# Channel 0 of b as a three-row product on TensorE, the copy of b's E on ScalarE, and two buffers for the products

## The chip, the cores and the metric

The kernel runs on one core of a Trainium2 chip. The metric is device time in microseconds of one execution, lower is better. The core's engines are TensorE (PE in the profile; PEld is its weight load), VectorE (DVE), ScalarE (ACT), GpSimd (POOL) and SyncE (SP), whose queue issues most transfers.

## The reference

The input x has 8 x 3072 x 256 numbers. Three stages follow each other:

```python
X = np.fft.fft(np.fft.fft(x, axis=1), axis=2).real    # stage 1
t = X.reshape(B * S, D)
t = ((t @ w_a) * (t @ w_b)) @ w_out                   # stage 2, F = 1536
# stage 3: 8 experts, the one with the largest logit per token
h = np.maximum(t[mask] @ w1[e], 0.0)
out[mask] = gate * (h @ w2[e])
```

## The kernel before, in words

The kernel makes use of a symmetry of the Fourier transform over the sequence: position s and position -s have spectra over the 256 channels whose even parts agree and whose odd parts differ in sign. So stages 1 and 2 work on a half of the positions: there are 24 tiles of 512 positions (t = 0 to 23), and each product gives the rows of two positions. UV holds the transformed input of a batch, Wt the weights w_a and w_b after the same turn, both as a high and a low fp16 part. Wt[:, ab, uv, a] has 128 partitions for w_a (ab = 0) and w_b (ab = 1), for the even (uv = 0) and the odd part (uv = 1), high (a = 0) and low (a = 1).

The even part has 129 channels, one more than the partitions. The one that is left over, channel 0, sits in partition 0 of the odd part. It has to be taken out of the odd product and belongs to the even one. The kernel before does it on VectorE: x's row of that channel is spread over 128 partitions by two one-row matmuls per tile (line 817, kept in st_x), the weight's row is turned into one number per partition (w0, by ab_row), and x * w0 is added to the even product E, once for a and once for b (line 861).

The work goes by steps: for each tile twelve steps f, each for 128 of the 1536 columns of w_a and w_b, 288 in all. The order of all engines' instructions is written out by hand. In a step TensorE makes the even products (six matmuls with 512 columns, three for a and three for b, into banks s[0] and s[1]), then the second product of a step three back with w_out (24 matmuls with 256 columns, line 894), and then the odd products into the same banks (line 828 both times). Around it stand:

- first(): ScalarE copies b's bank to BP (line 834), VectorE makes AM, the first half of hf, and b minus (lines 835 to 837), for the step before;
- the pair of line 861 on VectorE, which moves E of a and of b from the banks of this step to EE, with channel 0 added. The odd products may not start before;
- first_minus(): VectorE makes the other half of hf (line 840);
- second(): ScalarE rounds hf to fp16 in hl (line 845), GpSimd makes the rest (line 847).

The products' tiles hf come from a pool of three buffers. from64_sizes takes its scratch tiles from the same pool while weights are converted in the setup. Other work is dealt into the steps by a planner with a budget per engine and step: Fourier products of later batches (line 662), folding x on GpSimd, splitting the expert weights, and for each tile, after its second products, the normalisation of rows (lines 930, 941, 947), transposes on SP's queue, the gate, and eight scatters on GpSimd. After the steps the expert stage follows, which the change doesn't touch. mini_rows does one extra tile of eight positions with small matmuls (line 771).

Of the kernel before, what the change touches and what calls it, by code (L numbers as in the profile page):

```python
# [8 lines left out]
FP32 = mybir.dt.float32  # L9
FP16 = mybir.dt.float16  # L10
BF16 = mybir.dt.bfloat16
I32 = mybir.dt.int32
ACTF = mybir.ActivationFunctionType
ALU = mybir.AluOpType
# [4 lines left out]
B, S, D = 8, 3072, 256  # L19
F = 1536  # L20
# [21 lines left out]
def chain_kernel(ctx, tc, x, x384, w_a, w_b, w_out, w_gate, w_og, w1, w2, dft, c16, c32, ids, out):  # L42
    nc = tc.nc
    w_a, w_b, w_out = (w.bitcast(I32).rearrange("a (b c) -> a b c", c=2) for w in (w_a, w_b, w_out))
    pe, act, dve, pool, sp = nc.tensor, nc.scalar, nc.vector, nc.gpsimd, nc.sync
# [34 lines left out]
    UV = place_at(H2, FP16, [2, 4, F], "p (a b c) -> p a b c", a=2, b=4)  # L80
    Wt = place_at(H2 + 24576, FP16, [2, 2, 2, F], "p (a b c d) -> p a b c d", a=2, b=2, c=2)
    wo = place_at(H2 + 49152, FP16, [NF, 2, D], "p (a b c) -> p a b c", a=NF, b=2)
    UVm = place_at(H2 + 64512, FP16, [4, 128], "p (a b) -> p a b", a=4)
# [15 lines left out]
    one = es.enter_context(tc.tile_pool(name="one", bufs=1))  # L99
    two = es.enter_context(tc.tile_pool(name="two", bufs=2))  # L100
    three = es.enter_context(tc.tile_pool(name="three", bufs=3))
# [4 lines left out]
    w0 = one.tile([128, 2, NF], FP32, name="w0")  # L106
# [20 lines left out]
    EE = one.tile([128, 2, 512], FP32, name="EE")  # L127
# [4 lines left out]
    sel = place_at(H2 + 60992, FP32, [48], None)[0:4 * B]  # L132
    junk = place_at(H2 + 63488, BF16, [2, D], "p (a d) -> p a d", a=2)
    AM = one.tile([128, 2, 512], FP32, name="AM")
    ohx = one.tile([128, 9, 8], FP16, name="ohx")
    sinv = one.tile([128, 2], FP32, name="sinv")
    Rt = one.tile([128, 12, 2], FP32, name="Rt")
# [29 lines left out]
    def at(u, point, fn):  # L167
        if fn is None:
            return
        todo.setdefault((u, point), []).append(fn)  # L170
# [72 lines left out]
    TINY = 1.125 * 2.0 ** -15  # L243

    def from64_sizes(raws):
        ts = [three.tile([128, 2, 512], I32, tag="hf", name="t64") for _ in raws]
        for t, raw in zip(ts, raws):
            act.activation(out=t[:, 1].bitcast(FP32), in_=raw[:, :, 1].bitcast(FP32), func=ACTF.Abs)
        return ts
# [42 lines left out]
    def ab_low(ab, m, ps):  # L292
        fs = slice(512 * m, 512 * m + 512)
        for uv in range(2):
            dve.scalar_tensor_tensor(out=Wt[:, ab, uv, 1, fs], in0=ps[uv], scalar=sw[ab], in1=Wt[:, ab, uv, 0, fs], op0=ALU.mult, op1=ALU.subtract)

    def ab_row(ab, m, ps):
        for f in range(4 * m, 4 * m + 4):
            for h in range(2):
                pe.matmul(out=ps[:, f:f + 1], lhsT=Wt[0:1, ab, 1, h, 128 * f:128 * f + 128], rhs=ones16[0:1, 0:1], start=(h == 0), stop=(h == 1))  # L300
        act.activation(out=w0[:, ab, 4 * m:4 * m + 4], in_=ps[:, 4 * m:4 * m + 4], func=ACTF.Copy)
# [450 lines left out]
    def mini_rows():  # L752
        st = {}
        n = B * NF
        Bm = place_at(Pb[1], FP32, [n], None)
        hm = place_at(Pb[1] + 4 * n, FP32, [n], None)
        hlm = place_at(Pb[1] + 8 * n, FP16, [2, NF, B], "p (a f n) -> p a f n", a=2, f=NF)

        def clear():
            pool.memset(Ym, 0.0)  # L760
            pool.memset(rowim, 0)
            pool.memset(ohm, 0.0)

        def prod():
            st["s"] = aux()
            for f in range(NF):
                for ab in range(2):
                    o = 128 * ab + B * f
                    for uv in range(2):
                        for i, (a, h) in enumerate(((0, 0), (0, 2), (1, 0))):  # L770
                            pe.matmul(out=st["s"][:, o:o + B], lhsT=Wt[:, ab, uv, a, 128 * f:128 * f + 128], rhs=UVm[:, h + uv, 0:B], start=(uv == 0 and i == 0), stop=(uv == 1 and i == 2))

        def copy_b():
            act.activation(out=Bm, in_=st["s"][:, 128:128 + n], func=ACTF.Copy)

        def times():
            dve.scalar_tensor_tensor(out=hm, in0=st["s"][:, 0:n], scalar=CA * CA, in1=Bm, op0=ALU.mult, op1=ALU.mult)

        def hi():
            act.activation(out=hlm[:, 0].rearrange("p f n -> p (f n)"), in_=hm, func=ACTF.Copy)  # L780

        def lo():
            dve.tensor_tensor(out=hlm[:, 1].rearrange("p f n -> p (f n)"), in0=hm, in1=hlm[:, 0].rearrange("p f n -> p (f n)"), op=ALU.subtract)

        def sums():
            st["y"] = aux()[0:B, 0:D]
            for f in range(NF):
                for i, (a, h) in enumerate(((0, 0), (1, 0), (0, 1))):
                    pe.matmul(out=st["y"], lhsT=hlm[:, h, f, :], rhs=wo[:, f, a, :], start=(f == 0 and i == 0), stop=(f == NF - 1 and i == 2))

        def copy_y():
            act.activation(out=Ym[0:B, 0, :], in_=st["y"], func=ACTF.Copy)

        return [
            (0, [("pool", 1.0, clear)]),
            (1, [("pe", 1, prod), ("act", 0.25, copy_b), ("dve", 0.2, times)]),
            (1, [("act", 0.25, hi), ("dve", 0.5, lo)]),
            (1, [("pe", 1, sums), ("act", 0.4, copy_y)]),
        ]
# [3 lines left out]
    st_x = {}  # L803
    prev = []

    def aux():
        return cur["aux"][0]
# [5 lines left out]
    def x_items(t):  # L813
        def spread():
            st_x["ps", t] = aux()
            for i, k in enumerate((1, 3)):
                pe.matmul(out=st_x["ps", t], lhsT=ones16[0:1, :], rhs=UV[0:1, (t // 3) % 2, k, 512 * (t % 3):512 * (t % 3) + 512], start=(i == 0), stop=(i == 1))

        def keep_x():
            st_x[t] = xes[t % 2]  # L820
            act.activation(out=st_x[t], in_=st_x["ps", t], func=ACTF.Copy)

        return [(0, [("pe", 1, spread), ("act", 0.6, keep_x)])]

    def products(s, src, fs, uv):
        for ab in range(2):
            for i, (a, h) in enumerate(((0, 0), (0, 2), (1, 0))):
                pe.matmul(out=s[ab], lhsT=Wt[:, ab, uv, a, fs], rhs=src[:, h + uv, :], start=(uv == 0 and i == 0), stop=(i == 2), skip_group_check=(uv == 1))  # L828

    def first(P):  # L830

        a, b = P["s"]
        P["hf"] = three.tile([128, 2, 512], FP32, tag="hf", name="hf")
        act.activation(out=BP, in_=b, func=ACTF.Copy)  # L834
        dve.scalar_tensor_tensor(out=AM[:, 0, :], in0=EE[:, 0, :], scalar=2.0, in1=a, op0=ALU.mult, op1=ALU.subtract)  # L835
        dve.scalar_tensor_tensor(out=P["hf"][:, 0, :], in0=a, scalar=CA * CA, in1=BP, op0=ALU.mult, op1=ALU.mult)  # L836
        dve.scalar_tensor_tensor(out=b, in0=EE[:, 1, :], scalar=2.0, in1=b, op0=ALU.mult, op1=ALU.subtract)  # L837
# [12 lines left out]
    def step(T, f, job):  # L850
        src = tile_src(T)
        fs = slice(128 * f, 128 * f + 128)
        s, cur["aux"] = SB[cur["n"] % 2], SB[(cur["n"] + 1) % 2]
        cur["n"] += 1
        run("sp")
        P = {"s": s, "T": T, "f": f}
        products(s, src, fs, 0)
        if prev:
            first(prev[0])
        for ab in range(2):  # L860
            dve.scalar_tensor_tensor(out=EE[:, ab, :], in0=st_x[T[0]], scalar=w0[:, ab, f:f + 1], in1=s[ab], op0=ALU.mult, op1=ALU.add)  # L861
        if prev:
            first_minus(prev[0])
        run("early")
        if job:
            g, i, k = job
            ps = dft_products(g, i, bank_beside(k))
            dft_out(g, i, ps)
            if i == 11:
                dft_last(g)  # L870
        middle()
        run("act")
        if prev:
            second(prev.pop())
        run("dve0")
        run("dve")
        run("pool0")
        run("pool")
        products(s, src, fs, 1)
        prev.append(P)  # L880

# [307 lines left out]
    for g, G in enumerate(GROUPS):  # L1189
# [4 lines left out]
        for b in G:  # L1194
            for t in range(3 * b, 3 * b + 3):
                ts = [(t, 0, 4)]
# [17 lines left out]
    for u, un in enumerate(plan):  # L1214
        if un[0] == "D":
            first_of.setdefault(un[1], u)
            if pending:
                T, f = pending.pop(0)
                if f == NF - 1:
                    ends[T] = u  # L1220
        else:
            begins.setdefault(un[1], u)
            pending.append((un[1], un[2]))
            if len(pending) > 3:
                T, f = pending.pop(0)
# [28 lines left out]
    with tc.manual_schedule():  # L1254
# [28 lines left out]
        raws = deque()  # L1283
# [28 lines left out]
        flat = [Y[n].rearrange("p a d -> p (a d)") for n in range(4)]  # L1312
# [70 lines left out]
        for m in range(3):  # L1383
            ab_row(0, m, flat[1])
        ab_low(1, 0, [flat[0], flat[2]])
        ab_row(1, 0, flat[1])
        warm(8)
        out_squares(0)
        sizes()
# [16 lines left out]
        for m in range(1, 3):  # L1406
            def late(m=m):
                late_ps.append(cur["aux"])
                ab_turn(1, m, H, late_ps[-1])
            at(m + 1, "pe", late)  # L1410
            at(m + 1, "dve", lambda m=m: ab_low(1, m, late_ps[m - 1]))
            at(m + 2, "pe", lambda m=m: ab_row(1, m, aux()))
            reserve(m + 1, "act", 1.2)
            reserve(m + 1, "dve", 1.2)
        at(4, "pool0", lambda: pool.memset(rows2[:, :, :, 258:264], 0))
# [6 lines left out]
        for T in tiles:  # L1422
            t, j0, _ = T
# [61 lines left out]
        for u, un in enumerate(plan):  # L1485
            if un[0] == "D":
                _, g, i, k, n = un
# [363 lines left out]
```

## Time and profile before

| what | value |
|---|---|
| median of 3 runs | 3058.04 us (3055.01 to 3067.98) |
| profiled execution: its own time | 3057.12 us |
| profiled execution: span | 3055.4 us |
| mean granted TensorE clock | 0.976 of full |
| TensorE, VectorE, ScalarE, GpSimd busy | 2881.0, 2209.5, 1315.1, 1335.7 us |

The profile comes from one execution. Its span is the time from the first to the last instruction; the device time lies a little above it. Busy time is a sum per engine; an engine that is busy most of the time needn't bound each stage.

### The profile page before, as it was taken

The numbers are of one execution on the slowest core, as the hardware profiler recorded it, in microseconds if no ns is written. First come the engines' busy times: TensorE is split into PE (matmuls) and PEld (weight loads), VectorE is DVE, ScalarE is ACT, GpSimd is POOL, SyncE is SP. The second block draws the span as 40 slices with busy tenths as digits, with TensorE's granted clock in tenths as the row PEclk, the third lists the DMA queues.
The fourth block names the chain that finished last, engine by engine and source line by source line (L and its number), as shares of the span: only waits on it lengthen the run. The fifth ranks groups of instructions, "written<-read, shape, count | busy, mean of one in ns | idle before, by whom it ended". The sixth has DMA issues, their size and how long they took to land.

```text
span 3055.4 us, 62396 instructions
## 1 busy us (share of the span) xinstructions
PE 2881.0 (94%) x24101; PEld 2184.9 (72%) x24101; DVE 2209.5 (72%) x4079; ACT 1315.1 (43%) x2605; POOL 1335.7 (44%) x1083
## 2 busy tenths in 40 slices
PE   6899899989999989999989999989999999999998
PEld 4466666656666756666666666678888888888898
DVE  8779699688999688999777998744555555555556
ACT  4454455545455445455444454432333333333332
POOL 6466587365775455775333445413211111111112
PEclk7899999999999999999999999999999999999999
DMA  5421722541221541221452212363222222222211
GB/s 190 118 60 43 177 74 60 145 107 40 77 76 47 137 116 46 77 72 46 99 126 84 77 50 82 87 186 98 58 51 51 50 53 52 51 53 51 51 44 35
DMA packets 363577, 244.48 MB, mean 80 GB/s; under 512 B 303101, under 2 KB 320669, under 8 KB 362382
## 3 DMA queue, kind: packets, MB, share of 16 engines
q1 hardware_dynamic: 342158, 184.75, 24.5%
q0 software_dynamic: 18816, 51.54, 4.9%
q10 hardware_dynamic: 2304, 4.20, 0.5%
q8 instruction: 188, 3.08, 0.4%
q14 instruction: 111, 0.91, 0.1%
HBM read 106.60 MB, written 70.33 MB: 58 GB/s over the span
## 4 chain that ended last, share of the span: by engine, by line
PE 75%; DVE 11%; issue 7%; DMA 3%; ACT 2%; POOL 0%; SPq 0%; DVEq 0%; POOLq 0%; ACTq 0%
PE s L828 19%; PE y L894 18%; PE g L1598 16%; PE g L1622 15%; PE s L662 3%; DVE EE L861 2%; DVE s L837 2%; DVE rows L947 1%; DVE hf L840 1%; DMA big<-in_dft_dram 1%; DVE AM L835 1%; DMA rows<-rows,di 1%; PE s L962 1%; ACT BP L834 1%; PE s L289 1%
## 5 line engine op out<-in xcount | busy, mean ns | idle before, releaser
L828 PE MATMUL s<-big 128*128 128x512 f16 x3456 | 824.9, 389 | 74.1 <-DVE EE L861 66.8
L847 POOL TENSOR_TENSOR hl<-hf,hl 128x1024 f16<-128x1024 f32 x288 | 626.4, 2175 | 566.2 <-ACT hl L845 422.9
L894 PE MATMUL y<-big,hl 128*128 128x256 f16 x6912 | 821.6, 273 | 1.0 <-POOL hl L847 1.0
L894 PEld LDWEIGHTS <-hl 128*128 128x128 f16 x6912 | 672.8, 98 | 152.0 <-issue 12.2
L828 PEld LDWEIGHTS <-big 128*128 128x128 f16 x3456 | 344.2, 100 | 448.4 <-issue 118.2
L1625 POOL DMA_INDIRECT out_dram<-o,di x189 | 195.4, 1034 | 777.3 <-ACT o L1624 524.8
L845 ACT ACTIVATE hl<-hf 128x1024 f16<-128x1024 f32 x288 | 303.8, 1055 | 499.2 <-DVE hf L840 434.3
L1598 PE MATMUL g<-yt,w1t 128*128 128x256 f16 (+1 forms) x4704 | 492.8, 265 | 3.5 <-DVE w1t L1579 3.5
L1622 PE MATMUL g<-w2t,hh 128*128 128x256 f16 x2896 | 479.5, 273 | 0.0
L1598 PEld LDWEIGHTS <-w1t 128*128 128x128 f16 x4704 | 432.0, 98 | 50.1 <-DVE w1t L1579 3.8
L1601 DVE SCALAR_TENSOR_TENSOR hl<-g,hh 128x512 f16<-128x512 f32 x378 | 260.3, 691 | 240.8 <-ACT hh L1600 239.9
L1622 PE MATMUL g<-w2t,hl 128*128 128x256 f16 x1448 | 394.7, 273 | 0.0
L1600 ACT ACTIVATE hh<-g 128x512 f16<-128x512 f32 x378 | 225.3, 598 | 276.3 <-PE g L1598 276.3
L1622 PEld LDWEIGHTS <-hh 128*128 128x128 f16 x3024 | 295.0, 98 | 33.7
L1050 POOL DMA_INDIRECT rows<-rows,di x192 | 191.7, 998 | 264.4 <-DMA rows<-rows,di 199.2
L836 DVE SCALAR_TENSOR_TENSOR hf<-s,BP 128x512 f32<-128x512 f32 x288 | 198.3, 688 | 112.9 <-ACT BP L834 102.7
L1583 DVE COPY w2t<-big 128x4104 f16 x98 | 120.5, 1229 | 206.7 <-PE g L1622 206.7
L1624 ACT ACTIVATE o<-g,sc 128x256 f32<-128x256 f32 x189 | 89.7, 474 | 409.6 <-PE g L1622 360.5
L835 DVE SCALAR_TENSOR_TENSOR AM<-EE,s 128x512 f32<-128x512 f32 x288 | 195.9, 680 | 30.7 <-PE s L828 28.3
L861 DVE SCALAR_TENSOR_TENSOR EE<-big,w,s 128x512 f32<-128x512 f32 x288 | 201.5, 741 | 0.0
L861 DVE SCALAR_TENSOR_TENSOR EE<-xe,w,s 128x512 f32<-128x512 f32 x288 | 201.4, 740 | 0.0
L834 ACT ACTIVATE BP<-s 128x512 f32<-128x512 f32 x288 | 170.2, 591 | 67.6 <-PE s L828 64.3
(332 smaller groups left out, 3039.5 us busy)
## 6 DMA issues: line engine op xcount, KB each, us to landing
big<-in_x_dram SPq DMA_DIRECT2D x48, 514.0 KB
big<-in_dft_dram SPq DMA_DIRECT2D x60, 384.0 KB
big<-in_moe_w_dram SPq DMA_DIRECT2D x16, 1024.0 KB
wsc<-big SPq DMA_DIRECT2D x32, 512.0 KB
big<-wsc SPq DMA_DIRECT2D x7, 2050.0 KB
big<-in_dft_dram SPq DMA_DIRECT2D x60, 192.0 KB
big<-wsc ACTq DMA_DIRECT2D x16, 256.2 KB
raw<-in_moe_w_out_dram SPq DMA_DIRECT2D x6, 512.0 KB
```

Source lines behind the costliest of these rows:

```text
L828: pe.matmul(out=s[ab], lhsT=Wt[:, ab, uv, a, fs], rhs=src[:, h + uv, :], start=(uv == 0 and i == 0), stop=(i == 2), skip_group_check=(uv = ...
L834: act.activation(out=BP, in_=b, func=ACTF.Copy)
L835: dve.scalar_tensor_tensor(out=AM[:, 0, :], in0=EE[:, 0, :], scalar=2.0, in1=a, op0=ALU.mult, op1=ALU.subtract)
L836: dve.scalar_tensor_tensor(out=P["hf"][:, 0, :], in0=a, scalar=CA * CA, in1=BP, op0=ALU.mult, op1=ALU.mult)
L845: act.activation(out=hl[:, 0], in_=hf, func=ACTF.Copy)
L847: pool.tensor_tensor(out=hl[:, 1], in0=hf, in1=hl[:, 0], op=ALU.subtract)
L861: dve.scalar_tensor_tensor(out=EE[:, ab, :], in0=st_x[T[0]], scalar=w0[:, ab, f:f + 1], in1=s[ab], op0=ALU.mult, op1=ALU.add)
L894: pe.matmul(out=Y[w // 2][:, w % 2, :], lhsT=hl[:, h, pm, 128 * j:128 * j + 128], rhs=wo[:, f, a, :], start=(f == 0 and i == 0 and w % 2 = ...
L1598: pe.matmul(out=ps[:, u, :], lhsT=w[:, a, q, 128 * f:128 * f + 128], rhs=yt[:, 2 * h + q, :], start=(m == 0), stop=(m == 5))
L1600: act.activation(out=hh[:, f0:f0 + nu, :], in_=ps, func=ACTF.Relu)
L1601: dve.scalar_tensor_tensor(out=hl[:, f0:f0 + nu, :], in0=ps, scalar=0.0, in1=hh[:, f0:f0 + nu, :], op0=ALU.max, op1=ALU.subtract)
L1622: pe.matmul(out=ps, lhsT=hx[:, f, ts], rhs=wv[:, a, f, :], start=(m == 0), stop=(m == 3 * NF2 - 1))
```

## The change

Channel 0 of b goes to TensorE. Its product is a sum of three rows: high weight by high x, high weight by low x, low weight by high x. b_row copies the weight's row from Wt to a tile W3 with three partitions (three transfers on SP's queue) and clears it in Wt, so that the odd product no longer contains it. x_rows does the same for x, with three transfers for each tile into X3, which lies in an unused part of AM, or X3m for the extra tile. products then adds a matmul with three rows to the even product of b. E of b needs nothing added and is copied to EE by ScalarE. Channel 0 of a stays as it was. The pool of hf has two buffers instead of three.

```diff
     AM = one.tile([128, 2, 512], FP32, name="AM")
+    X3 = AM[0:3, 1, :].bitcast(FP16).rearrange("p (a n) -> p a n", a=2)
+    W3 = one.tile([3, F], FP16, name="W3")
+    X3m = one.tile([3, 8], FP16, name="X3m")
...
-        ts = [three.tile([128, 2, 512], I32, tag="hf", name="t64") for _ in raws]
+        ts = [two.tile([128, 2, 512], I32, tag="hf", name="t64") for _ in raws]
...
+    def b_row(m):
+
+        fs = slice(512 * m, 512 * m + 512)
+        for i, h in enumerate((0, 0, 1)):
+            sp.dma_start(out=W3[i:i + 1, fs], in_=Wt[0:1, 1, 1, h, fs])
+        dve.memset(Wt[0:1, 1, 1, :, fs], 0.0)
+
+    def x_rows(src, n, dst):
+        for i, h in enumerate((1, 3, 1)):
+            sp.dma_start(out=dst[i:i + 1, 0:n], in_=src[0:1, h, 0:n])
...
         def clear():
+            x_rows(UVm, B, X3m)
...
-                            pe.matmul(out=st["s"][:, o:o + B], lhsT=Wt[:, ab, uv, a, 128 * f:128 * f + 128], rhs=UVm[:, h + uv, 0:B], start=(uv == 0 and i == 0), stop=(uv == 1 and i == 2))
+                            pe.matmul(out=st["s"][:, o:o + B], lhsT=Wt[:, ab, uv, a, 128 * f:128 * f + 128], rhs=UVm[:, h + uv, 0:B], start=(uv == 0 and i == 0), stop=(ab == 0 and uv == 1 and i == 2))
+                    if ab:
+                        pe.matmul(out=st["s"][:, o:o + B], lhsT=W3[:, 128 * f:128 * f + 128], rhs=X3m[:, 0:B], start=False, stop=True)
...
         def keep_x():
+            x_rows(UV[:, (t // 3) % 2, :, 512 * (t % 3):512 * (t % 3) + 512], 512, X3[:, t % 2])
...
-    def products(s, src, fs, uv):
+    def products(s, src, fs, uv, x3=None):
...
-                pe.matmul(out=s[ab], lhsT=Wt[:, ab, uv, a, fs], rhs=src[:, h + uv, :], start=(uv == 0 and i == 0), stop=(i == 2), skip_group_check=(uv == 1))
+                pe.matmul(out=s[ab], lhsT=Wt[:, ab, uv, a, fs], rhs=src[:, h + uv, :], start=(uv == 0 and i == 0), stop=(i == 2 and (uv == 1 or ab == 0)), skip_group_check=(uv == 1))
+            if ab and not uv:
+                pe.matmul(out=s[ab], lhsT=W3[:, fs], rhs=x3, start=False, stop=True)
...
-        P["hf"] = three.tile([128, 2, 512], FP32, tag="hf", name="hf")
+        P["hf"] = two.tile([128, 2, 512], FP32, tag="hf", name="hf")
...
-        products(s, src, fs, 0)
+        products(s, src, fs, 0, X3[:, T[0] % 2, :])
...
-        for ab in range(2):
-            dve.scalar_tensor_tensor(out=EE[:, ab, :], in0=st_x[T[0]], scalar=w0[:, ab, f:f + 1], in1=s[ab], op0=ALU.mult, op1=ALU.add)
+        dve.scalar_tensor_tensor(out=EE[:, 0, :], in0=st_x[T[0]], scalar=w0[:, 0, f:f + 1], in1=s[0], op0=ALU.mult, op1=ALU.add)
+        act.activation(out=EE[:, 1, :], in_=s[1], func=ACTF.Copy)
...
-        ab_row(1, 0, flat[1])
+        b_row(0)
...
-            at(m + 2, "pe", lambda m=m: ab_row(1, m, aux()))
+            at(m + 2, "pe", lambda m=m: b_row(m))
```

## Rows read from the trace of the kernel before

**Rows 1.** The page, part 1: busy time, share of the span, instructions.
```profile
PE 2881.0 (94%) x24101; PEld 2184.9 (72%) x24101; DVE 2209.5 (72%) x4079; ACT 1315.1 (43%) x2605; POOL 1335.7 (44%) x1083
```

**Rows 2.** Busy time by stretches: PE, PEld, DVE, ACT, POOL, clock, DMA share, GB/s.
```profile
86.00:1975.00 1889.00, 1768.60 (x13571) 1200.51 (x13571) 1583.73 (x3067) 934.00 (x1902) 1064.09 (x813) 0.98 0.32 84
...
2060.00:3055.00 995.00, 982.81 (x9456) 885.28 (x9453) 520.79 (x805) 310.93 (x561) 204.38 (x199) 1.00 0.23 55
```

**Rows 3.** The chain that ended last, 715 to 730 us: start, us, what.
```profile
718.93 2.59 PE s L828 x12
721.52 2.62 PE y L894 x24
```

**Rows 4.** Waits, 86 to 1975 us: us in total, times, longest us.
```profile
PE s L828 <- DVE EE L861: 66.8, 34, 6.1
```

**Rows 5.** Timelines of VectorE and TensorE, 762 to 802 us: start, us, instructions.
```profile
784.47 7.48 DVE L947 SCALAR_TENSOR_TENSOR rows<-tail,r,rows 128x256 f16<-128x256 f32 x3
...
795.11 4.72 PE L828 MATMUL s<-big 128*128 128x512 f16 x12 [6.09 <-DVE EE L861]
```

**Rows 6.** Timeline of all engines, 715 to 738 us.
```profile
720.20 2.14 POOL L847 TENSOR_TENSOR hl<-hf,hl 128x1024 f16<-128x1024 f32 x1 [3.09 <-ACT hl L845]
720.33 0.60 ACT L834 ACTIVATE BP<-s 128x512 f32<-128x512 f32 x1 [0.21 <-PE s L828]
...
721.03 0.69 DVE L836 SCALAR_TENSOR_TENSOR hf<-s,BP 128x512 f32<-128x512 f32 x1 [0.28 <-ACT BP L834]
...
721.64 0.69 DVE L837 SCALAR_TENSOR_TENSOR s<-EE,s 128x512 f32<-128x512 f32 x1
...
722.24 1.40 DVE L861 SCALAR_TENSOR_TENSOR EE<-big,w,s 128x512 f32<-128x512 f32 x2
...
723.55 0.68 DVE L840 SCALAR_TENSOR_TENSOR hf<-s,AM 128x512 f32<-128x512 f32 x1
...
723.98 2.75 PE L828 MATMUL s<-big 128*128 128x512 f16 x12
...
726.18 0.69 DVE L836 SCALAR_TENSOR_TENSOR hf<-s,BP 128x512 f32<-128x512 f32 x1 [0.17 <-ACT BP L834]
```

**Rows 7.** The chain that ended last, 1278 to 1300 us.
```profile
1280.52 1.31 PE y L894 x12
1281.83 0.53 PE s L817 x2
1282.36 1.42 PE y L894 x12
...
1298.33 0.43 PE s L388 x2
1298.77 1.31 PE y L894 x12
```

**Rows 8.** Busy time of the step behind the longest stall, columns as in rows 2.
```profile
795.11:802.29 7.18, 7.18 (x36) 4.00 (x36) 7.15 (x14) 2.58 (x4) 4.58 (x4) 0.72 0.42 115
```

**Rows 9.** The page, costliest groups: busy us, mean ns, idle before, releaser.
```profile
L845 ACT ACTIVATE hl<-hf 128x1024 f16<-128x1024 f32 x288 | 303.8, 1055 | 499.2 <-DVE hf L840 434.3
...
L834 ACT ACTIVATE BP<-s 128x512 f32<-128x512 f32 x288 | 170.2, 591 | 67.6 <-PE s L828 64.3
```

**Rows 10.** Busy time of twelve steps, 692.72 to 757.46 us, columns as in rows 2.
```profile
703.14:708.35 5.21, 5.21 (x38) 3.53 (x36) 4.16 (x8) 5.00 (x15) 4.97 (x7) 1.00 0.01 2
...
718.77:723.98 5.21, 5.21 (x38) 3.53 (x36) 4.93 (x10) 4.58 (x11) 2.14 (x1) 1.00 0.36 70
...
sum 64.74, PE 64.74 PEld 43.87 DVE 56.19 ACT 36.79 POOL 35.31; mean PE 5.39 PEld 3.66 DVE 4.68 ACT 3.07 POOL 2.94
```

**Rows 11.** Transfers by line: median us from issue to landing at the end.
```profile
rows<-rows,di POOLq DMA_INDIRECT x192, 2.5
```

**Rows 12.** The chain that ended last, 78 to 110 us.
```profile
86.93 5.35 DMA raw<-in_moe_w_out_dram
```

## What the change was predicted to do

> **What bounds the kernel now.** I read the page first, then busy time by stretches, the chain of work that ended last, the waits, and last the timelines of a few steps. On the page TensorE is busy 94% of the span [rows 1]; that is a mean over stages, so the next view cuts the span. The products of x with w_a and w_b, which the change touches, run from 86 to 1975 us. There TensorE is busy 1768.6 of 1889 us and VectorE 1583.7. Behind 2060 us comes another kernel half, in which TensorE is busy 982.8 of 995 us and nothing is changed [rows 2]. So the whole change happens in 1889 us with 288 steps.
>
> The chain shows what a calm step is. It consists of TensorE alone: twelve 512-column products in 2.59 us, then 24 matmuls of the second product in 2.62 us, then the next twelve [rows 3]. The step is 2.59 + 2.62 = 5.21 us, TensorE leaves no gap, and one 512-column matmul costs 2.59 / 12 = 0.216 us on the chain. This is the pattern of most steps. The exceptions are the 34 times that TensorE's products wait for VectorE's EE: 66.8 us in all, 6.1 the longest [rows 4]. The longest of them shows the kind: three subtractions of line 947 take 7.48 us on VectorE, and TensorE stands for 6.09 us. What follows costs too: the twelve products behind that stall take 4.72 us [rows 5] instead of 2.75 [rows 6].
>
> So TensorE bounds most steps, VectorE a few dozen. The change takes work from the second and gives some to the first.
>
> **What TensorE gets.** Each of 288 steps gets one matmul of 512 columns whose weights have three rows, between products of 128 rows (before it) and the second product's of 128 rows (behind it). The nearest rows are the pair of one-row matmuls of 512 columns that spreads x (line 817). In the chain that pair takes 0.53 us, and the twelve matmuls behind it 1.42 instead of 1.31: 0.53 + 0.11 = 0.64 us. The pair of line 388 has 512 columns too, but 128 rows: 0.43 us, that is 2 x 0.216, and the twelve behind it stay at 1.31 [rows 7]. The difference, 0.64 - 0.43 = 0.21 us, is paid once for going from 128 rows to one and back. The lower bound for the new matmul is thus 0.216 us (if three rows switch for nothing) and the upper 0.216 + 0.21 = 0.42. I take the upper: three rows are like one row and unlike 128, and in every step the new matmul stands alone between full ones, so it pays both borders for itself. 288 x 0.42 = 121 us, if every step is bound by TensorE.
>
> The rows above show the borders; a rule that speaks of them is in the Trainium skill, TensorEngine Tiling (Array Packing), Key Properties: changing the tiling mode drains the engine, whereas moving to another tile within a mode does not. The same skill's TensorE: Matmul & The Clock Gate says in its closing table (Why this matters for your kernels) that a single matmul with 32 rows takes as long as one with 128. By the second rule alone the sum would be 288 x 0.216 = 62 us; the first, and the rows of line 817, make it 121.
>
> The small product of eight columns (line 771) gets twelve three-row ones as well. Of their price the columns are next to nothing, 8 / 512 of 0.216; the borders make 12 x 0.21 = 3 us.
>
> **What VectorE loses.** One of the two EE instructions. The pair starts at 722.24 and the next instruction at 723.55 [rows 6]: 0.655 us each, 288 x 0.655 = 189 us of busy time. In a calm step this is worth nothing: the pair ends about 723.6, before TensorE comes back to the banks at 723.98. It counts only where VectorE is late. There each late step gets 0.66 us back from the instruction that is gone, and the comparison shifts by another 0.42 us as TensorE's own step grows: 1.08 us per late step. With one late step before each of the 34 stalls that is at most 34 x 1.08 = 37 us; some stalls are shorter than 1.08, others have two or three late steps before them. I take 34 us. Behind the long stalls the slower products go: 4.72 - 2.75 = 2.0 us each, where the granted clock over the step was 0.72 of full speed, between the levels of 1.2 and 2.4 GHz [rows 5, 8]. My estimate is eleven of these, 22 us, as the stage's mean clock of 0.98 leaves no more than some 38 us for all slow stretches [rows 2]. If stalls shrink, about 14 of the 22 come back. Together 48 us of at most 66.8 + 22 = 89. The 7.48 us themselves are not cured: the subtractions are slow there, not EE.
>
> **What ScalarE gets.** A copy of a bank per step, as BP is: 0.59 us, 170 us in all [rows 9]. It lies beside TensorE's second product, so it costs nothing by itself. Its place in the queue matters. It stands right behind BP and may only run when VectorE's line 837 has read the old EE. From the timeline: BP starts at 720.33, line 836 at 721.03, line 837 at 721.64 and ends about 722.25 [rows 6]; the copy would end about 722.9. From BP's start to the copy's end pass 2.6 us in which ScalarE does 1.2 us of work; before, the other work of the step ran there. Of a step of 5.63 us, 2.6 and the 1.06 of the hl copy [rows 9] are taken; about 1.85 us are left for everything else after a little latency. In one tile's steps ScalarE is busy 5.00 and 4.58 us [rows 10]; without BP and hl (1.65) that is 3.35 and 2.93. Each overruns by 1.5 and 1.1 us. What is queued behind: hl, then the next BP, for which VectorE waits with line 836. The next BP can be late by the time from EE's end to TensorE's return: one EE less, 722.9 instead of 723.6, against 723.98 + 0.42 = 724.4, so 1.5 us. Two overruns with a lighter step between add up to about 2.2, so 0.7 us reach TensorE per tile, 24 x 0.7 = 17 us; a little of that falls into stalls that are there anyway. I take 15, between 0 and 45.
>
> **Two buffers.** VectorE may write hf when GpSimd has read the one two steps before. GpSimd's subtraction that starts at 720.20 ends at 722.34, and line 836 of two steps later comes at 726.18 [rows 6]: 3.8 us to spare, and a longer step gives more. Cost nothing; if GpSimd's scatters took the cover, see the rivals. In the setup the same buffers hold the converted weights; VectorE uses them in its own order, so nothing.
>
> **The moved rows.** Three small transfers for each of 24 tiles, asked for two steps or more before the tile begins, on SP's queue; a small transfer lands in 2.5 us by the nearest row [rows 11]. Hidden behind those steps, more than 10 us; uncovered they would cost one landing per tile, 60 us. The three blocks of b's row replace 24 one-column matmuls, less than 1 us on the chain. Only the first has no cover: VectorE clears the row when the transfers have landed, some 3 us, and the conversion of w_out and its loads, which set the end of the setup (5.35 us of one load stand in the chain [rows 12]), move with it. Plus 3 us.
>
> **Sum.** 121 + 3 + 15 + 3 - 48 = 94 us. The profiled execution took 3057.1 us with a span of 3055.4; the median of three is 3058.0, 0.9 more. 3058 + 94 = 3152 us.
>
> **The rivals.**
> A: the change of rows costs nothing, three rows switch freely. For it: no row has three rows; against it: line 817 in the chain. 62 us instead of 121; VectorE then gains 0.88 instead of 1.08 per late step, so 42 come back, and ScalarE has less room, 25: 62 + 3 + 25 + 3 - 42 = 51, 3109 us. By the second page rule quoted above this would be the outcome.
> B: ScalarE's order becomes the bound. If no overrun is made up, 1.5 + 1.1 = 2.6 us per tile, 62 us, and only 22 us come back: 121 + 6 + 62 - 22 = 167, 3225 us. For it, the 5.00 of a 5.21 us step; against it, the mean of a tile, 3.07 us of 5.39 [rows 10].
> C: the missing third buffer makes VectorE wait for GpSimd while that issues scatters. Four steps of a tile hold two each; if each is late by half a microsecond (a guess, as no row shows such a wait), 96 steps make 48 us: 3200. Against it the 3.8 us above.
> D: faster. The three-row matmul runs beside its neighbours and costs TensorE nothing; then the relief decides: 48 - 15 - 6 = 27 us, 3031. It turns at 48 / 288 = 0.17 us per step, and no 512-column row is below 0.216.
>
> **How the numbers follow.** My forecast 0.70, A 0.12, B 0.08, C 0.05, D 0.03, and 0.02 that gains and costs cancel. I predict 3152. Its own bounds: with all 89 us back and ScalarE free, 121 + 6 - 89 = 38, 3096; with ScalarE at 45 and 25 back, 121 + 6 + 45 - 25 = 147, 3205. The range 3092 to 3203 holds those, A and C, and leaves out B and D. What differs by under 0.5% (15 us) can hardly be told from no change here: faster 0.03, same 0.02, slower 0.95.
>
> **What would show it.** In the chain a calm step of 5.63 us: twelve products and the new matmul in two pieces, the first of the 24 late by about 0.1 us. Rival A would show 5.43. One EE of line 861 left on VectorE, its busy time down by some 190 us; the waits of TensorE for EE at half or less; ScalarE up by 170 us, and some waits of line 836 for BP that are longer than before. TensorE's wait for the copy on ScalarE should be rare. I am wrong if calm steps stay below 5.4 us, or if the stage is paced by ScalarE or GpSimd.

## The result and the profile after

The changed kernel takes 3096.99 us (median of 4 runs, 3095.82 to 3102.04) against 3056.53 us before (4 runs): a ratio of 1.0136, with a 95% interval of 1.0117 to 1.0154. It is slower by 40 us, as forecast in sign, but by less than half of the 94 us predicted. The time lies inside the range (3092 to 3203), close to its lower end, where nearly all lost time of TensorE had been assumed to come back.

First the page of the kernel after, part 1, and then, of the same kernel, the windows of the stage with the products (columns as in [rows 2]).

```profile
PE 2981.1 (96%) x24377; PEld 2184.4 (71%) x24377; DVE 1987.1 (64%) x3794; ACT 1459.4 (47%) x2890; POOL 1339.6 (43%) x1083
```

```profile
86.00:2019.00 1933.00, 1873.99 (x13922) 1206.64 (x13923) 1363.08 (x2789) 1086.11 (x2210) 1066.81 (x816) 0.99 0.31 83
```

Against [rows 1] VectorE has lost 222 us of busy time, although only 189 us of instructions were taken from it. That surplus of 33 us is the first hint. In the stage TensorE is idle for 1933.00 - 1873.99 = 59 us; in [rows 2] it was 120.

Next the chain of the kernel after around 700 us: start, us, what.

```profile
698.63 2.59 PE s L846 x12
701.22 0.32 PE s L848
701.54 2.73 PE y L914 x24
704.27 2.59 PE s L846 x12
```

This is the predicted calm step of [rows 3]: 2.59 + 0.32 + 2.73 = 5.64 us by these rounded rows (5.63 by the starts of the odd products in 162 of the 287 steps) instead of 5.21. The three-row matmul shows 0.32 and the 24 behind it 0.11 more than the 2.62 of before; over the step that is 5.63 - 5.21 = 0.42. The upper bound, taken from the one-row pair, was right.

Now the waits, 86 to 2019 us: the row that answers to [rows 4], then the idle time of the weight loads in front of the new matmul (132.1 / 288 = 0.46 us each, for which the profile shows no releaser), and three rows of ScalarE's order.

```profile
PE s L846 <- DVE EE L880: 15.2, 15, 1.9
...
PEld L848 <- issue: 132.1, 288, 8.7
...
DVE hf L856 <- ACT BP L854: 182.6, 236, 2.3
...
ACT EE L881 <- DVE s L857: 457.3, 278, 4.8
...
ACT BP L854 <- PE s L846: 155.3, 152, 3.8
```

TensorE's waits for EE fell from 66.8 us in 34 to 15.2 in 15, far below the half that the prediction allowed for. ScalarE's copy waits for line 857 as foreseen, and VectorE's wait for BP grew from 102.7 us (151 times) to 182.6 (236), but no wait of TensorE for the copy on ScalarE shows.

The step that stalled longest before, [rows 5], took 795.11 - 783.65 = 11.46 us. Its counterpart is a calm step. The timeline of the kernel after, VectorE and GpSimd (start, us, instruction):

```profile
796.19 0.68 DVE L860 SCALAR_TENSOR_TENSOR hf<-s,AM 128x512 f32<-128x512 f32 x1
796.79 1.27 DVE L967 SCALAR_TENSOR_TENSOR rows<-tail,r,rows 128x256 f16<-128x256 f32 x3
...
794.24 2.15 POOL L867 TENSOR_TENSOR hl<-hf,hl 128x1024 f16<-128x1024 f32 x1
796.61 1.00 POOL L1070 DMA_INDIRECT rows<-rows,di  x1 [0.22 <-DMA rows<-rows,di]
799.58 2.12 POOL L867 TENSOR_TENSOR hl<-hf,hl 128x1024 f16<-128x1024 f32 x1 [1.98 <-ACT hl L865]
```

The same three subtractions of row_lo that took 7.48 us now take 1.27. Between 796.4 and 799.6 GpSimd issues a scatter and then waits; no computing instruction of its own runs. Before, it looked like this (the trace of the kernel before, GpSimd, the same place):

```profile
777.63 2.15 POOL L847 TENSOR_TENSOR hl<-hf,hl 128x1024 f16<-128x1024 f32 x1
779.95 1.00 POOL L1050 DMA_INDIRECT rows<-rows,di  x1 [0.17 <-issue]
782.75 0.98 POOL L1050 DMA_INDIRECT rows<-rows,di  x1 [1.80 <-DMA rows<-rows,di]
783.75 2.15 POOL L847 TENSOR_TENSOR hl<-hf,hl 128x1024 f16<-128x1024 f32 x1
786.06 1.00 POOL L1050 DMA_INDIRECT rows<-rows,di  x1 [0.17 <-issue]
787.08 2.14 POOL L847 TENSOR_TENSOR hl<-hf,hl 128x1024 f16<-128x1024 f32 x1
789.17 1.28 POOL L519 TENSOR_TENSOR big<-big 128x512 f32<-128x512 f32 x1
790.39 1.26 POOL L520 TENSOR_TENSOR big<-big 128x508 f32<-128x508 f32 x1
791.60 0.40 POOL L521 COPY big<-big 128x4 f32<-128x4 f32 x1
```

Here GpSimd was still in one hl when row_lo began at 784.47, and went straight on with a scatter, the next hl and the three instructions of a fold of x. The 7.48 us of row_lo end at 791.95, 0.3 us behind line 520. Over the whole kernel, all rows of row_lo (min/median/max in ns), before and then after:

```profile
L947 DVE SCALAR_TENSOR_TENSOR rows<-tail,r,rows x192: 462/479/5442, 204.2 to 1993.4; 128x256 f16<-128x256 f32 x192
```

```profile
L967 DVE SCALAR_TENSOR_TENSOR rows<-tail,r,rows x192: 471/480/2616, 206.2 to 2027.2; 128x256 f16<-128x256 f32 x192
```

The usual time is 0.48 us in both; the longest, 5.44 before, is one of the three in the stall above. Read one by one, 32 of the 192 instructions of row_lo take over 1 us before, and each of the 32 ends 0.28 or 0.29 us behind the end of a computing instruction of GpSimd. After, 5 do. Above the median these 32 take 60.6 us, and the 5 after 6.2. Before, 26 of the 32 end behind an hl; after, none does, and all 5 end behind the second instruction of a fold.

This accounts for most of the waits, not for all: of the 34 waits of TensorE for EE before, 18 with 47.3 of the 66.8 us end within 6 us behind a slow row_lo; after, 2 of 15 with 3.6 of 15.2 us. What the others, 19.5 us before and 11.6 after, come from was not looked into.

Where the 40 us of span (3055.4 to 3095.5) come from, by starts of the odd products of line 828 and line 846:

| stretch | before | after | difference |
|---|---|---|---|
| start to the second step's odd products | 105.6 | 104.8 | -0.8 |
| from there to the last step's | 1864.6 | 1897.6 | +33.0 |
| rest of that step, tail, experts | 1085.1 | 1093.0 | +7.9 |

The middle stretch by busy time, before and then after (columns as in [rows 2]):

```profile
105.60:1970.20 1864.60, 1753.69 (x13434) 1189.94 (x13435) 1566.13 (x3026) 924.87 (x1879) 1061.96 (x812) 0.98 0.32 84
```

```profile
104.80:2002.40 1897.60, 1849.87 (x13716) 1187.81 (x13717) 1345.10 (x2747) 1068.41 (x2164) 1060.58 (x812) 0.99 0.31 83
```

TensorE's idle time falls from 110.9 to 47.7 us, by 63. Its busy time grows by 96 us, not by the 121 that the new matmul costs, as the slow products behind the stalls go as well: 25 us, of which 22 are in the products of line 828, 818.0 us before and 796.4 after. So of the 121 us, 63 + 25 = 88 come back.

### The profile page after: what moved, and what is told of

Read it like the earlier page. It is cut to its first block, busy times and chain, and to the rows that moved or that the text cites. A ratio compares the mean times of both kernels' runs of the same rounds, so it can differ in the third digit from the quotient of the medians.

```text
span 3095.5 us, 63026 instructions
## 1 busy us (share of the span) xinstructions
PE 2981.1 (96%) x24377; PEld 2184.4 (71%) x24377; DVE 1987.1 (64%) x3794; ACT 1459.4 (47%) x2890; POOL 1339.6 (43%) x1083
## 4 chain that ended last, share of the span: by engine, by line
PE 82%; DVE 5%; issue 4%; DMA 4%; ACT 3%; SPq 1%; POOL 0%; POOLq 0%; DVEq 0%; ACTq 0%
PE y L914 22%; PE s L846 21%; PE g L1618 16%; PE g L1642 15%; PE s L676 3%; PE s L848 3%; DMA big<-in_dft_dram 1%; DMA rows<-rows,di 1%; DVE s L857 1%; PE s L982 1%; ACT big L950 1%; ACT hl L865 1%; PE y L676 0%; ACT big L704 0%; ACT BP L854 0%
## 5 line engine op out<-in xcount | busy, mean ns | idle before, releaser
L867 POOL TENSOR_TENSOR hl<-hf,hl 128x1024 f16<-128x1024 f32 x288 | 619.2, 2150 | 621.0 <-ACT hl L865 583.7
L846 PE MATMUL s<-big 128*128 128x512 f16 x3456 | 803.8, 382 | 22.0 <-DVE EE L880 15.2
L914 PEld LDWEIGHTS <-hl 128*128 128x128 f16 x6912 | 649.1, 98 | 145.9 <-issue 70.2
L881 ACT ACTIVATE EE<-s 128x512 f32<-128x512 f32 x288 | 171.9, 597 | 465.0 <-DVE s L857 457.3
L856 DVE SCALAR_TENSOR_TENSOR hf<-s,BP 128x512 f32<-128x512 f32 x288 | 198.7, 690 | 183.2 <-ACT BP L854 182.6
L857 DVE SCALAR_TENSOR_TENSOR s<-EE,s 128x512 f32<-128x512 f32 x288 | 197.3, 685 | 0.0
```

Of the source, the lines that this page charges most:

```text
L867: pool.tensor_tensor(out=hl[:, 1], in0=hf, in1=hl[:, 0], op=ALU.subtract)
L914: pe.matmul(out=Y[w // 2][:, w % 2, :], lhsT=hl[:, h, pm, 128 * j:128 * j + 128], rhs=wo[:, f, a, :], start=(f == 0 and i == 0 and w % 2 = ...
```

## The experiments

Three theories were put against each other. **Relief**: the waits went because VectorE lost an instruction. **Pace**: they went because TensorE's step became longer. **Collision**: VectorE's late steps come from row_lo waiting for GpSimd, and the step's length decides whether they meet. Each run is given as its median against the kernel before in the same set of runs (3057.14 us for the first four, 3053.41 for the next four, 3060.00 for the last three).

**One part of the change at a time.** The first widens the new matmul to 128 partitions, the added rows zero.

```diff
-    X3 = AM[0:3, 1, :].bitcast(FP16).rearrange("p (a n) -> p a n", a=2)
-    W3 = one.tile([3, F], FP16, name="W3")
+    X3 = AM[:, 1, :].bitcast(FP16).rearrange("p (a n) -> p a n", a=2)
+    W3 = one.tile([128, F], FP16, name="W3")
```

> The changed kernel, but the tiles of channel 0 have 128 partitions of which 125 hold zeros, so that the extra matmul has 128 rows like its neighbours. If the borders between row counts cost 0.21 us per step, a calm step falls from 5.63 to 5.42 us, and 288 x 0.21 = 60 us go: about 3037 us, or some 20 more if the shorter step lets TensorE's waits for VectorE come back. If the three-row matmul itself is what is slow, nothing moves: 3097.

Measured: 3054.79 us, ratio 0.9989 (0.9977 to 1.0001): -2, where the three-row form has +40. The borders between three and 128 rows are really paid; of their 288 x 0.21 = 60 us 43 are gained, as the waits for EE rise again to 25.8 us (24 times) with the shorter step. This is also a test of rival A's sum: at a step of 5.43 us it gave +51, and -2 is measured. The sum is off by 53 us without the borders and by 54 with them, so the error isn't in the borders.

The second gives VectorE its EE instruction for b back, with a factor of zero, and leaves the three-row matmul.

```diff
+        dve.memset(w0, 0.0)
...
-        act.activation(out=EE[:, 1, :], in_=s[1], func=ACTF.Copy)
+        dve.scalar_tensor_tensor(out=EE[:, 1, :], in0=st_x[T[0]], scalar=w0[:, 1, f:f + 1], in1=s[1], op0=ALU.mult, op1=ALU.add)
```

> The changed kernel, but E of b stays on VectorE, with its instruction as before and a number that is zero, so that VectorE has as much work as before and TensorE as much as after. Theory of relief (the stalls went because VectorE lost an instruction): they stay, TensorE waits for EE some 50 us and the time is about 3150. Theory of pace (they went because TensorE's step is 0.42 us longer): waits of 20 us at most, about 3100.

Measured: 3108.36 us, ratio 1.0156 (1.0127 to 1.0184): +51. Its wait of TensorE for EE:

```profile
PE s L847 <- DVE EE L881: 17.1, 15, 2.7
```

VectorE has all its old work, and the waits have gone all the same, from 66.8 to 17.1 us. That speaks against relief.

The third keeps everything but the three-row matmuls in the steps, so channel 0 of b is missing in the even product.

```diff
-            if ab and not uv:
-                pe.matmul(out=s[ab], lhsT=W3[:, fs], rhs=x3, start=False, stop=True)
```

> The changed kernel without the three-row matmuls in the steps: channel 0 of b is left out of the even product. ScalarE copies E of b, VectorE has the shorter step, TensorE the work of before, a calm step is 5.21 us. Theory of relief: the stalls stay away and the 121 us go, about 2976. Theory of pace: with the step of before most of the stalls and of the slow products behind them are back, about 3030 to 3050.

Measured: 3038.44 us, ratio 0.9933 (0.9908 to 0.9957): -19. Its wait of TensorE for EE and its chain near 700 us:

```profile
PE s L846 <- DVE EE L878: 59.8, 52, 6.9
```

```profile
702.35 0.70 DVE s L855
703.11 0.04 issue
703.15 0.60 ACT EE L879
703.75 0.41 ACT big L948 x2
704.18 0.52 ACT big L948 x2
...
706.85 0.95 ACT hl L863
707.80 0.49 ACT BP L852
```

VectorE lost its instruction here, and the waits for EE hardly moved (59.8 us in 52). Only 14 row_lo are over 1 us, so a new cause stands in: with a step of 5.21 us the chain near 700 us runs through ScalarE, from VectorE's line 855 over the copy, the squares and hl to BP, for which VectorE waits. That is the mechanism of rival B, at a step without the extra matmul.

The fourth is the kernel before with two buffers for hf.

```diff
-        P["hf"] = three.tile([128, 2, 512], FP32, tag="hf", name="hf")
+        P["hf"] = two.tile([128, 2, 512], FP32, tag="hf", name="hf")
```

> The kernel before with two buffers for the products and nothing else. If GpSimd always reads them in time, no change, 3057 within 8 us. If VectorE waits for GpSimd while that issues scatters, 20 to 50 us more, and a wait of the first half of hf for GpSimd shows in the waits.

Measured: 3059.49 us, ratio 1.0011 (0.9997 to 1.0025). The buffers cost nothing that can be told from no change; rival C falls.

**The step's length alone.** Both of the next keep VectorE's two EE instructions. In one the extra matmul has 128 partitions, in the other there are two more such matmuls of zeros per step.

```diff
+                for k in range(2):
+                    pe.matmul(out=s[ab], lhsT=Z3, rhs=x3, start=False, stop=False)
```

> The changed kernel with the extra matmul widened to 128 partitions (the added rows are zeros) and with VectorE keeping its EE instruction for b (its factor for b is zero), so VectorE's work per step is that of the kernel before and only TensorE's step grows, by 0.216 us to about 5.42. Pace theory (a longer step lets VectorE arrive in time): TensorE's waits for EE fall from 66.8 to 30-45 us, and of the 62 us that 288 x 0.216 would cost about half comes back: 3068 to 3080 us. Relief theory (the waits go because VectorE loses an instruction): the waits stay near 60, 3105 to 3115 us.

> The same, with two more matmuls of 128 partitions and zero weights in each step: three extra in all, a calm step of about 5.86 us. Pace theory: hardly any wait for EE is left to be removed, so the waits fall to 5-15 us and the time rises by nearly the full price of the last 0.23 us per step over the one with a three-row matmul and VectorE's EE kept (3108): 3155 to 3175 us; against the kernel before that is +100 to +118 instead of 288 x 0.65 = 187. Relief theory: the waits stay above 40 us, 3215 to 3235 us.

Measured: 3081.0 us, ratio 1.0091 (1.0074 to 1.0108), and 3157.83 us, ratio 1.035 (1.0332 to 1.0367). Both are on the side of pace, the first just above its bracket. The chains show the steps, of the first and then of the second:

```profile
564.09 2.59 PE s L849 x12
566.68 0.22 PE s L851
566.90 2.62 PE y L917 x24
```

```profile
1406.55 2.59 PE s L851 x12
1409.13 0.43 PE s L854 x2
1409.57 0.22 PE s L855
```

and the waits of the first and of the second:

```profile
PE s L849 <- DVE EE L883: 39.1, 30, 5.3
```

```profile
PE s L851 <- DVE EE L887: 11.6, 11, 2.2
```

With the kernel before and the second experiment this makes a series in which VectorE's and ScalarE's work in a step stays the same and TensorE's step grows (the changed kernel's transfers and two buffers apart):

| calm step, us | price, 288 x 0.216, 0.42 or 0.65 | time | given back | waits for EE | row_lo over 1 us |
|---|---|---|---|---|---|
| 5.21 (before) | 0 | 0 | 0 | 66.8 | 32 |
| 5.43 (one, 128 rows) | 62 | +27.6 | 34 | 39.1 | 17 |
| 5.63 (one, three rows) | 121 | +51.2 | 70 | 17.1 | 7 |
| 5.86 (three, 128 rows) | 187 | +104.4 | 83 | 11.6 | 3 |

What comes back, the waits and the slow row_lo move together. The first 0.42 us of a longer step cost less than half their price; behind them it is paid nearly in full: of the last 66 us only 13 came back.

**The collision itself.** One run leaves out GpSimd's folds of x for batches 1 to 7 (their Fourier products use batch 0's values). The same two lines stand in both functions of the fold:

```diff
+                if b:
+                    return
```

> The kernel before with GpSimd's folding of x left out for batches 1 to 7 (their Fourier products use batch 0's values), all else as it was. Collision theory (VectorE's late steps come from its instructions with two operands in SBUF, row_lo above all, running several times slower while GpSimd works): the waits for EE fall from 66.8 to below 30 us, row_lo's mean from 818 ns to below 620, and the time to 2985-3015 us. Load theory (VectorE is late because it is given too much work in a step): the waits and row_lo's slow instructions stay, 3050 to 3060 us.

Measured: 3018.12 us, ratio 0.9887 (0.987 to 0.9903). Waits for EE 47.3 us (27 times), row_lo's mean 702 ns. This is half of what the collision theory expected: not the folds alone, GpSimd's hl and scatters are left, and 23 row_lo are still over 1 us. But the load theory, 3050 to 3060, is out: VectorE's work is unchanged here.

The next leaves all work in place and only issues GpSimd's scatters one per step in place of two, for tiles 6 to 20.

```diff
         for w in range(0, nt, 2):
+            if 6 <= t < 21:
+                for k in range(w, min(w + 2, nt)):
+                    items.append((1, [("pool0", 1.3, scatter(k))]))
+                continue
             items.append((1, [("pool0", 1.3, scatter(w))] + ([("pool", 1.3, scatter(w + 1))] if w + 1 < nt else [])))
```

> The kernel before with one scatter per step in place of two for tiles 6 to 20, so that GpSimd's own work is spread otherwise; same work. Collision theory: GpSimd waits less for its scatters and runs in shorter bunches, the waits for EE fall to 40-55 us and the time to 3025-3045 us. Load theory: the same time, 3050 to 3060 us.

Measured: 3018.49 us, ratio 0.9884 (0.9868 to 0.9901), better than expected. Its waits of TensorE and of GpSimd, then row_lo in the groups by line (columns as in [rows 9]):

```profile
PE s L828 <- DVE EE L861: 42.6, 32, 3.5
...
POOL rows L1050 <- DMA rows<-rows,di: 151.6, 56, 7.2
```

```profile
L947 DVE SCALAR_TENSOR_TENSOR rows<-tail,r,rows 128x256 f16<-128x256 f32 x192 | 110.0, 623 | 0.0
```

GpSimd's waits for its scatters to land fell from 199.2 us (82 times, the kernel before) to 151.6, row_lo's mean from 818 to 623 ns, and only 13 of its instructions are over 1 us; 11 of these lie before 540 or after 1890 us, where no scatters of the edited tiles run. A line's order on an engine that is busy for 44% of the span was worth 35 us on TensorE. This version computes all of the reference and beats both kernels.

The rows of GpSimd suggest why both the order and the step's length matter; no run tests this by itself. Where two scatters stand between two hl, as from 777.63 to 783.75 above, 6.12 us pass from one hl to the next, since the second scatter waits 1.80 us for the first one's transfer. There are 50 such pairs in the kernel before (without a fold between them), with a median of 6.11 us, 50 in the changed kernel, none below 5.98, and 13 in this run. A calm step of 5.21 us is 0.9 us shorter, one of 5.63 us 0.5 and one of 5.86 us 0.25. By so much GpSimd falls behind in each of these steps, until its hl lies where row_lo runs.

If longer steps and other scatters remove the same stalls, the second must be worth less the longer the step is. The same edit was made to the widened form of the change (step 5.43) and to the change itself (5.63):

> The changed kernel with the extra matmul widened to 128 partitions, and one scatter per step in tiles 6 to 20. If the longer step and the other order of scatters remove the same stalls (pace and collision are one cause), little is left for the second to remove: 3030 to 3048 us, against 3055 without it. If they remove different stalls, the 35 us add up: 3015 to 3025 us.

> The changed kernel with one scatter per step in place of two in tiles 6 to 20, nothing else. If the longer step already keeps VectorE's late instructions clear of GpSimd, the order of the scatters is worth little here: 3085 to 3098 us against 3097. If the two remove different stalls: 3055 to 3068 us.

Measured: 3045.24 us, ratio 0.9959 (0.9945 to 0.9974), and 3094.71 us, ratio 1.0113 (1.0096 to 1.0129). The scatters' order is worth 35 us at 5.21, 12 at 5.43 (-14.8 against -2.4 without it) and 6 at 5.63 (+34.7 against +40.5; the kernel before itself differs by as much between the sets). So it is in the main one cause.

The last writes zeros in row_lo, so that the low half of each row is left out and the instruction reads one operand from SBUF instead of two.

```diff
-                    dve.scalar_tensor_tensor(out=rowt[:, w, 256:512], in0=Yt[:, w, :], scalar=st["r"][:, w:w + 1], in1=rowt[:, w, 0:256], op0=ALU.mult, op1=ALU.subtract)
+                    dve.tensor_scalar(out=rowt[:, w, 256:512], in0=Yt[:, w, :], scalar1=0.0, scalar2=None, op0=ALU.mult)
```

> The kernel before with row_lo writing zeros: one operand from SBUF in place of two, so the low half of each row is left out; the count and size of the instructions stay. Collision theory (an instruction of VectorE that reads two operands from SBUF waits until GpSimd has finished the one it is in): no row_lo over 1 us is left, the waits for EE fall from 66.8 to below 30 us, 2995 to 3020 us. If any instruction of VectorE from SBUF to SBUF waits for GpSimd, or VectorE is just too full: 3050 to 3060 us with row_lo's longest still above 3 us in the first of these.

Measured: 3005.84 us, ratio 0.9827 (0.9811 to 0.9843); waits for EE 40.5 us (31 times). Its row_lo (min/median/max):

```profile
L947 DVE TENSOR_SCALAR rows<-tail x192: 272/283/6169, 203.8 to 1944.0; 128x256 f16<-128x256 f32 x192
```

The time is in the collision theory's bracket, but not for its reason. The instruction became shorter, 283 instead of 477 ns, which alone takes 37 us from VectorE; and 16 of the 192 are still over 1 us, one of 6.17, each ending 0.15 to 0.18 us behind the end of a GpSimd instruction. So the collision theory was too narrow in its second half: not only instructions with two operands in SBUF wait, this one-operand form does too. How much of the 54 us is the shorter instruction and how much the fewer waits, the run doesn't separate.

## Why the prediction was right in sign and wrong in size

**What TensorE gets: right.** 0.42 per step was predicted and stands in the chain; 121 us are the price. The widened form shows 0.22 for the matmul and no border, and gains 43 us of their 60.

**What VectorE loses: this is the step that failed.** It priced what comes back at 48 of at most 89 us, by two assumptions: that a late step gets at most its 1.08 us back, and that the 7.48 us "are not cured: the subtractions are slow there, not EE". The subtractions were not slow; they waited for GpSimd. Such a delay doesn't shrink by 0.42 when the step grows by 0.42; where the two no longer meet, it vanishes whole, and so do the slow products behind it. Priced by the prediction's own split, the 0.42 of the longer step were worth 48 x 0.42 / 1.08 = 19 us; the second experiment, with the longer step and all of VectorE's work, shows 121 - 51 = 70 back (65 to 82 by its interval). These 70 - 19 = 51 us are most of the 54 by which the sum was off. In the changed kernel itself the stage gives back 88 us, whatever ScalarE's copy costs already taken off: nearly all of the 89 that the prediction had set as the most.

The other share, the lost instruction against ScalarE's copy, came out about right: 48 - 19 = 29 of relief less 15 for ScalarE, a net 14 us, were in the sum, and copying on ScalarE instead of VectorE measured 51.2 - 40.5 = 11 us at the changed kernel's step (the two intervals, 39 to 56 and 36 to 47 us, overlap, so this size is loose). Its value depends on the step, too: 30 us at 5.43 (+27.6 against -2.4), 19 at 5.21.

The behaviour could have been looked for. The Trainium skill, SBUF — State Buffer, section Who interferes with whom, says that a VectorE instruction with two inputs in SBUF contends with a GpSimd instruction that reads SBUF, and that the later one is blocked until the earlier has finished; also that tensor_scalar can contend in a fast mode. The trace agrees that both forms can wait: 32 of 192 row_lo above 1 us, each ending 0.28 or 0.29 us behind a GpSimd instruction, and 16 of the one-operand form, whose 283 ns against 477 fit a faster mode, though no row names the mode. On who waits, and for how long, the trace differs from it (last section). The sign of it stood in the row: three equal instructions of 0.48 us that took 7.48.

**What ScalarE gets: the mechanism is real, but at the wrong step.** VectorE's waits for BP grew as foreseen (102.7 to 182.6 us), and in the run without the three-row matmul the chain goes through ScalarE's order. The change seems to give ScalarE the room it needs with its own 0.42: in the changed kernel TensorE has no wait for the copy, and the chain of a calm step is TensorE's alone. The 15 us put down for ScalarE were not isolated by any run; they are part of the 11 us above.

**The small product: right.** Each of its twelve parts takes about 0.5 us in the changed kernel, against 3.75 / 12 = 0.31 before: some 2.3 us, where 3 were predicted.

**Two buffers: right**, no cost that can be told from nothing (1.0011). **The moved rows:** +3 was predicted, -0.8 measured up to the second step. The first three-row matmul waits 7.9 us for its transfer, but the two matmuls of line 348 behind it, which had waited 9.5 us for VectorE's sum (ss), now wait 3.3: one wait took the place of another.

**Not foreseen:** +7.9 us behind the last step. The same stretch lies between 1081 and 1092 us over all kernels of this study, taken from the last product's start (1084.1 before, 1092.0 after), so how much of it the change causes stays open.

**Rivals.** A (no borders) falls by the chain and the widened form. B and C are told above. D, which ends on the faster side, set the turn at 0.17 us per step. Without the matmul the kernel is 19 us faster and with 0.22 us per step the same as before (0.9989), so the turn lies near 0.2. Two slips in the sums change nothing here: the upper bound of 3205 lies just outside the range to 3203 that is said to hold it, and A's sum keeps 3 us for borders that cost nothing in A.

## What to carry to other kernels

An instruction that took several times its usual duration was waiting for something here; find what ends with such an instruction before pricing what cures it. A stall made by a meeting of two engines is removed whole by a shift, so an addition to the bounding engine can cost less than half its own time, until few stalls are left, and then it costs nearly all of it. For the same reason such a kernel is better served by moving the other engine's work: the order of the scatters alone gave 35 us here, while the longer step only hid the same stalls at a higher price.

## What the runs showed of the hardware

- VectorE's row_lo takes 0.48 us, or until 0.28 to 0.29 us behind the end of a computing instruction of GpSimd: up to 5.44 us, over three such instructions that follow each other without a gap (787.08 to 791.65 us). It isn't always held for the whole run of them: in the kernel before, the last of three row_lo from 287.10 us ends at 291.01, 0.28 us behind an hl, while the fold's line 529 is already running. What decides this is not shown.

```profile
287.10 3.91 DVE L947 SCALAR_TENSOR_TENSOR rows<-tail,r,rows 128x256 f16<-128x256 f32 x3
...
288.42 2.31 POOL L847 TENSOR_TENSOR hl<-hf,hl 128x1024 f16<-128x1024 f32 x1
290.69 0.92 POOL L529 TENSOR_TENSOR big<-big 128x258 f32<-128x258 f32 x1
```

- Who starts first by the profile doesn't decide: the row_lo of 5.44 us starts at 786.50, GpSimd's hl at 787.08, 0.58 us later, behind a scatter. In the kernel before, 12 of the 32 slow row_lo are such cases: the computing instruction starts 0.51 to 0.58 us behind them, where 0.48 us would have been enough for them to end.
- In the changed kernel three row_lo run at full speed (1.27 us) while GpSimd issues a scatter (796.61 to 797.61): issuing as such doesn't hold VectorE. In the kernel before, 44 row_lo overlap a scatter and no computing instruction, and take 0.48 us.
- A matmul of three rows between matmuls of 128 costs 0.42 us per step, the same with 128 rows 0.21 to 0.22.
